# Attention and SiLU feed-forward in one kernel: output-weight rows regrouped, and the second batch's products moved into the first slab's second pass

## The chip, the cores and the metric

The kernel runs on one core of one Trainium2 chip. The metric is the device time of one launch in microseconds (us). Five engines work side by side, each on its own queue in program order: TensorE (PE in the profile, with its weight loads as PEld), VectorE (DVE), ScalarE (ACT), GpSimd (POOL) and SyncE (SP), which here only issues transfers. Sixteen DMA engines move the data.

## The reference, cut to what matters

```
q_s = exp(q) / sum over d            # 8 batches, 8 heads, 576 tokens, 64 wide
k_s = exp(k) / sum over tokens
kv  = k_s^T v                        # per batch and head, 64 x 64
x   = q_s kv, heads side by side     # 4608 tokens x 512
h   = x @ w_in                       # 512 x 2048
g   = h * sigmoid(beta * h)          # beta: one number for each of 2048 units
out = g @ w_out                      # 2048 x 512
```

(The maxima that the reference subtracts ahead of each exponential cancel in the quotients, and the kernel leaves them out.) All inputs and the output are float32; the matmuls run in bf16.

## The kernel before, in words

**Slabs and passes.** The 4608 tokens are nine slabs of 512. Slab t below 8 holds the first 512 tokens of batch t; slab 8 collects the last 64 of all batches. For each slab, pass 1 computes the hidden units: 16 tiles f of 128 units, each four matmuls over m (the four head pairs, 128 of the 512 features), 64 matmuls into PSUM banks 0 to 2 in turn. ACT turns each tile into GT with SiLU. Pass 2 multiplies GT with the output weights WOUT: four token groups u of 128, 16 matmuls each, again 64. The copies to O2S (`o2_evac`) and one store of 1 MB follow.

**Attention of a batch.** Heads are handled in pairs hp = 0 to 3. ACT makes EQ = exp(q) and EK = exp(k), where the two heads of a pair lie on partitions 0 to 63 and 64 to 127, so EK takes two instructions for each pair. DVE sums and scales EQ (`norm_main`, its product sometimes on POOL). PE transposes EQ into QT (`t_steps`; from batch 2 on a DMA does it). V is cast to bf16 in VB (`cast_v`). PE multiplies EK with VB over nine groups of 64 tokens (`kv_steps` or `kv_now`, nine matmuls for each pair); DVE scales the result by the reciprocal key sums into KVD (`kvd`); PE multiplies KVD with QT (`out_mm`), and the copy of that (`out_now`, `out_step`) is XT, which pass 1 of the batch's slab reads.

**How order is set.** Instructions are recorded once, in the order of the program, and each engine runs its own in that order. `Program.plan` derives semaphore waits from named keys (a tile's part, a PSUM bank). Attention of later batches is laid between the matmuls of the passes by hand: `tick()` counts matmuls in `slot`, and a list `todo` of pairs (tick, step) is worked off as the count passes. In slab 0 ticks 9 to 64 are pass 1 and ticks 65 to 128 are pass 2; `spread(steps, lo, hi)` distributes steps over ticks. Every matmul is recorded by `mm`, so all carry its line, L349, and can be told apart by their tiles: XT,WIN is pass 1, WOUT,GT pass 2, VB,EK the k-v products, QT,KVD and QTR,KVD the attention outputs (the latter for the 64 remaining tokens of two batches), IDB,EQ a transpose (L347), WARM a matmul on zeros that occupies PE during the head.

**The head.** SP issues q of batch 0 in four parts, beta, k and v in four parts each (L251, L522, L261). POOL issues the input weights in eight chunks of 256 columns, cast to bf16 by the transfer (`load_win`, L547), the first once k's third part has landed. Then come the output weights in four loads of 1 MB (`load_wout`, L532), gated by `wgate`: SP waits until W_in's chunk 4 of 0 to 7 has landed. They are staged as float32 in WST and O2S, and DVE scales them by 1/beta (RB) into WOUT (`scale_wout`). After them SP issues q, k and v of batch 1 in four parts each, the remaining q rows (QRF) and batch 2.

**Slab 0, pass 2.** The four token groups advance together, f by f, in banks 3 to 6. Batch 1's transposes of one pair each stand at ticks 109, 113, 117 and 121, its k-v products of pair 0 at tick 125. The other three pairs, the out matmuls and the copies of groups 0 and 1 follow behind pass 2, mixed with the first three tiles of slab 1 (`first_tiles`).

**Slab 1.** ACT makes the exponentials of batches 2 and 3 while PE runs pass 2; batch 2's k-v steps stand at ticks 97 to 108 and its outs at 112 to 124 (`attn_late`).

Of the kernel before, what the change touches and what calls it, by code (L numbers as in the profile page):

```python
# [14 lines left out]
D = 64  # L15
# [12 lines left out]
HS = S * D  # L28

# [127 lines left out]
def bass_efficient_attn_shen__then__act_swish_beta_kernel(  # L157
# [12 lines left out]
    with ExitStack() as es:  # L170
        def sb(name, shape, dt):
# [28 lines left out]
        BT = sb("BT", [NF, 128], F32)  # L200
# [4 lines left out]
        IDF = sb("IDF", [NF, NF], F32)  # L205
# [18 lines left out]
        add(POOL, lambda e: e.tensor_scalar(IDF[:, :], IOTA[0:NF, 0:NF], 0.0, None, ALU.is_equal),  # L224
            r=["iota"], w=["idf"])
        add(ACTE, lambda e: e.activation(DUMMY[:, 0:1], WARM[:, 0:1], ACT.Exp), r=["warm"],
            w=["dummy"])
# [10 lines left out]
        homes(0)  # L238

# [7 lines left out]
        def load_main(name, th, bufs, b, split=1):  # L247
            i = b % 2
            n = H // split
            for c in range(split):  # L250
                add(SP, lambda e, c=c: e.dma_start(dst(bufs[i], c * n, n), src(th, b, c * n, n)),  # L251
                    w=[(name, i, hp) for hp in range(c * n // 2, (c + 1) * n // 2)],
                    slot=f"{name}{i}_{c}")

        def load_pairs(name, th, bufs, b, split=1):
            i = b % 2
            n = NHP // split
            for c in range(split):
# [12 lines left out]
        def load_k(b, split=1):  # L271
            load_pairs("kf", kt_h, KF, b, split)

        def load_v(b, split=1):
            load_pairs("vf", vt_h, VF, b, split)
# [7 lines left out]


# [8 lines left out]
        def exp_k(b, hp0=0, n=4, step=1):  # L293
            i = b % 2
            for hp in range(hp0, hp0 + n, step):
                hps = range(hp, hp + step)
                for e_ in range(2):
# [5 lines left out]
                        r=[("kf", i, h) for h in hps], w=[("ek", i, h, e_) for h in hps])  # L303

# [26 lines left out]
        def cast_v(b, hp, eng=POOL):  # L331
            i = b % 2
            o = bass.AP(VB[i], hp * NG * VW, [[NHP * NG * VW, 128], [VW, NG], [1, 64]])
            a = bass.AP(VF[i], hp * KW, [[NHP * KW, 128], [64, NG], [1, 64]])
            add(eng, lambda e: (e.copy if eng == ACTE else e.tensor_copy)(o, a),  # L335
                r=[("vf", i, hp), ("vone", i)], w=[("vb", i, hp)])
# [133 lines left out]
        def attn_late(b):  # L470
            s = spread(kv_steps(b, (0, 1, 2, 3)), 97, 108)
# [3 lines left out]
            return s + spread(x, 112, 124)  # L475
# [17 lines left out]
        def ksum_inv(b, kb):  # L493
            i = b % 2
            add(DVE, lambda e: e.reciprocal(RC[i][:, :], PS[kb][:, 0:NHP]), r=[("ps", kb)],
                w=[("rc", i, hp) for hp in range(NHP)], bank=[kb])

        def kv_now(b, hp, bk, ks):
            i = b % 2
            for j in range(NG):  # L500
                l, r_, ke, kv, ko = kv_rows(b, hp, j)
                mm(PS[bk][:, 0:D + ks], l, r_[:, 0:D + ks], j == 0, j == NG - 1,
                   r=ke + kv + ko, w=[("ps", bk)], bk=bk)
            if ks:
                add(DVE, lambda e: e.reciprocal(RC[i][:, hp:hp + 1], PS[bk][:, D:D + 1]),
                    r=[("ps", bk)], w=[("rc", i, hp)], bank=[bk])
            kvd(b, hp, bk, 0)
# [8 lines left out]
        def go(steps):  # L516
# [4 lines left out]
        load_main("qf", qt_h, QF, 0, split=4)  # L521
        add(SP, lambda e: e.dma_start(BT[:, :], bass.AP(beta_h, 0, [[128, NF], [1, 128]])),  # L522
            w=["bt"], slot="bt")
        load_k(0, 4)
        load_v(0, 4)
# [4 lines left out]
        def load_wout(c):  # L530
            a = bass.AP(wout_h, 512 * c * DM, [[DM, 128], [128 * DM, 4], [1, DM]])
            add(SP, lambda e: e.dma_start(STAGE[c][:, :, :], a), w=SKEY[c],  # L532
# [12 lines left out]
        def load_win(c):  # L545
            a = bass.AP(win_h, 256 * c, [[DFF, 128], [128 * DFF, NM], [1, 256]])
            add(POOL, lambda e, c=c, a=a: e.dma_start(WIN[:, :, 256 * c:256 * c + 256], a),  # L547
                w=[("win", c)], slot=f"win{c}", after=P.writer[("kf", 0, 2)] if c == 0 else ())
            if c == 4:
                wgate.append(P.ops[-1])  # L550

        def read_beta():
            bb = bank(HEAD)
            mm(PS[bb][:, 0:NF], BT[:, :], IDF[:, :], True, True, r=["bt", "idf"],
               w=[("ps", bb)], bk=bb, tr=True)
            add(DVE, lambda e: e.tensor_scalar(BC[:, :], PS[bb][:, 0:NF], -1e-20, None,
                                               ALU.is_gt),
                r=[("ps", bb)], w=["bc0"], bank=[bb])
            add(DVE, lambda e: e.scalar_tensor_tensor(BC[:, :], PS[bb][:, 0:NF], 1e-20, BC[:, :],
# [3 lines left out]
                                                      PS[bb][:, 0:NF], ALU.mult, ALU.add),  # L563
                r=["bc", ("ps", bb)], w=["beta"], bank=[bb])
            add(DVE, lambda e: e.reciprocal(RB[:, :], BETA[:, :]), r=["beta"], w=["rb"])

        warm(8, 0)
# [4 lines left out]
        load_win(1)  # L572
# [5 lines left out]
        for c in range(2, 8):  # L578
            load_win(c)
        homes(1)  # L580
        exp_k(0)
# [7 lines left out]
        read_beta()  # L589
        cast_v(0, 0, DVE)  # L590
        warm(2, 0)
        ksum(0, 2, kb)
        cast_v(0, 1, DVE)
        go(t_steps(0, (3,), HEAD))
        warm(1, 0)
        ksum(0, 3, kb)
        ksum_inv(0, kb)
        cast_v(0, 2, ACTE)
        cast_v(0, 3, ACTE)
        warm(1, 0)  # L600
        add(ACTE, lambda e: e.activation(DUMMY[:, 1:2], WARM[:, 0:1], ACT.Silu), r=["warm"],
            w=["dummy"])

        hrot = [0]
        orot = [0]

        def pass1_mm(t, f, m, bk):
            x = XT8 if t == 8 else XT[t % 2]
            rd = [("xt8", p_) for p_ in range(4)] if t == 8 else [("xt", t % 2, m)]
            mm(PS[bk][:, :], WIN[:, m, 128 * f:128 * f + 128], x[:, m, :], m == 0,  # L610
               m == NM - 1, r=rd + [("win", f // 2)], w=[("ps", bk)], bk=bk)
# [4 lines left out]

        def first_tiles(t, n):
            bks = [HB[(hrot[0] + k) % 3] for k in range(n)]
            hrot[0] += n
# [194 lines left out]
```

## Time and profile before

| | us |
|---|---|
| median of 7 runs | 290.8 |
| lowest and highest of them | 290.34, 1037.62 |
| the profiled execution | 290.88 |
| its span | 289.05 |
| PE busy | 277.4 (96%) |
| ACT, DVE, POOL busy | 180.9, 111.8, 40.9 |
| first XT,WIN matmul | 16.69 |
| first WOUT,GT matmul of slab 0, of slab 1 | 30.71, 63.99 |
| last O2S copy begins | 285.22 |

Times inside the profile count from the span's start. PE is the engine that is nearly always busy, so what matters is where it isn't: idle time of another engine costs nothing by itself. A group's line gives its count, total and mean duration in ns, then the idle time of the engine before it and what ended it. In the timeline, the bracket at a line's end names the wait before it and its releaser. DMA queue q1 carries what SP and ACT issue, q0 what POOL issues, and q8 instruction fetches.

### The profile page before, as it was taken

How to read it: one execution, taken by the hardware profiler on the slowest of the kernel's cores; microseconds unless marked ns; L12 is line 12 of the kernel's file. 1: busy time of each engine (PE TensorE's matmuls, PEld its weight loads, DVE VectorE, ACT ScalarE, POOL GpSimd, SP SyncE). 2: the span in 40 equal slices, each digit the busy share in tenths (PEclk: the TensorE clock that was granted, in tenths of full speed). 3: DMA queues.
4: the chain of work that ended last, by engine and by line, in shares of the span. 5: the costliest groups of instructions: out<-in, count | busy, mean ns of one | idle time of the engine just before them, and what ended most of it. 6: DMA issues, size and time to landing. Idle time of an engine off the chain costs nothing.

```text
span 289.1 us, 3858 instructions
## 1 busy us (share of the span) xinstructions
PE 277.4 (96%) x1563; PEld 130.5 (45%) x1594; DVE 111.8 (39%) x205; ACT 180.9 (63%) x247; POOL 40.9 (14%) x60
## 2 busy tenths in 40 slices
PE   6889998999999999999999999999999999999994
PEld 2544443344444444444454445444544444444441
DVE  4731596207675157304660555054804300110011
ACT  5988469789987973689278926892660076017500
POOL 5770013033504030400040000000000000000000
PEclk9999999999999999999999999999999999999999
DMA  6999999995799999905990015000810030012022
GB/s 208 311 178 323 382 379 292 404 384 142 185 383 237 373 327 397 84 0 160 371 214 1 2 80 137 2 1 42 181 16 0 0 147 0 0 65 83 0 73 73
DMA packets 44306, 47.97 MB, mean 166 GB/s; under 512 B 20208, under 2 KB 32512, under 8 KB 43264
## 3 DMA queue, kind: packets, MB, share of 16 engines
q1 hardware_dynamic: 39744, 45.10, 50.7%
q0 software_dynamic: 4224, 2.10, 5.6%
q10 hardware_dynamic: 320, 0.52, 0.5%
q8 instruction: 12, 0.20, 0.3%
q14 instruction: 6, 0.05, 0.1%
HBM read 36.71 MB, written 9.44 MB: 160 GB/s over the span
## 4 chain that ended last, share of the span: by engine, by line
PE 77%; DMA 8%; SPq 6%; ACT 3%; issue 2%; POOL 2%; DVE 1%
PE PS L349 77%; DMA VF<-in_v_dram 4%; SPq L251 3%; DMA WIN<-in_moe_w_in_dram 2%; DMA KF<-in_k_dram 2%; SPq L261 2%; ACT EK L302 2%; SPq L532 1%; POOL WIN L547 1%; ACT EQ L290 1%; DVE O2S L650 0%; ACT L307 0%; POOL EQ L319 0%; DVE KVD L386 0%; ACT GT L613 0%
## 5 line engine op out<-in xcount | busy, mean ns | idle before, releaser
L613 ACT ACTIVATE GT<-PS,BETA 128x512 bf16<-128x512 f32 x144 | 98.3, 687 | 79.4 <-PE PS L349 79.3
L349 PE MATMUL PS<-XT,WIN 128*128 128x512 bf16 x562 | 130.8, 379 | 1.2 <-ACT XT L512 0.4
L349 PE MATMUL PS<-WOUT,GT 128*128 128x512 bf16 x562 | 131.2, 379 | 0.7
L349 PEld LDWEIGHTS PS<-XT,WIN 128*128 128x128 bf16 x576 | 55.4, 98 | 64.9 <-ACT GT L613 1.0
L349 PEld LDWEIGHTS PS<-WOUT,GT 128*128 128x128 bf16 x576 | 54.3, 98 | 62.4 <-DVE O2S L650 0.2
L650 DVE COPY O2S<-PS 128x512 f32<-128x512 f32 x34 | 23.2, 686 | 111.3 <-PE PS L349 111.3
L302 ACT ACTIVATE EK<-KF 64x1152 bf16<-64x1152 f32 (+1 forms) x40 | 38.7, 967 | 1.2 <-DMA KF<-in_k_dram 0.2
L349 PE MATMUL PS<-VB,EK 128*128 128x65 bf16 (+2 forms) x324 | 37.2, 190 | 2.0 <-POOL VB L335 1.0
L335 POOL CAST VB<-VF 128x576 bf16<-128x576 f32 x28 | 20.9, 745 | 74.6 <-PE PS L349 41.6
L349 PEld LDWEIGHTS PS<-VB,EK 128*128 128x128 bf16 x324 | 22.8, 97 | 10.0 <-POOL VB L335 2.3
L290 ACT ACTIVATE EQ<-QF 128x512 bf16<-128x512 f32 x32 | 18.2, 620 | 8.5 <-DMA QF<-in_q_dram 8.0
L317 DVE TENSOR_REDUCE QS<-EQ 128x8 f32<-128x512 bf16 (+1 forms) x22 | 20.1, 916 | 3.3 <-ACT EQ L290 3.1
L424 DVE CAST XT<-PS 128x512 bf16<-128x512 f32 x23 | 15.8, 691 | 11.5 <-PE PS L349 11.5
L319 DVE TENSOR_TENSOR EQ<-EQ,QI 128x1024 bf16<-128x1024 bf16 (+1 forms) x15 | 16.2, 1077 | 0.5
L349 PE MATMUL PS<-QT,KVD 128*128 128x512 bf16 x30 | 11.4, 380 | 0.5 <-DVE KVD L386 0.4
L319 POOL TENSOR_TENSOR EQ<-EQ,QI 128x512 bf16<-128x512 bf16 x7 | 7.3, 1044 | 31.4 <-DVE QI L318 31.2
L349 PE MATMUL PS<-WARM 128*128 128x512 bf16 x20 | 8.6, 548 | 1.2 <-DVE WARM L219 1.2
L386 DVE TENSOR_TENSOR KVD<-PS,RC 64x64 bf16<-64x64 f32 (+1 forms) x28 | 8.6, 308 | 1.1 <-PE PS L349 0.3
L325 DVE TENSOR_REDUCE QRS<-EQR 128x8 f32<-128x512 bf16 x4 | 2.7, 679 | 14.1 <-ACT EQR L307 14.1
L537 DVE TENSOR_SCALAR WOUT<-WST,RB 128x512 bf16<-128x512 f32 x8 | 3.3, 482 | 12.2 <-DMA WST<-in_moe_w_out_dram 12.2
L547 POOL DMA_DIRECT2D WIN<-in_moe_w_in_dram x8 | 6.2, 799 | 2.2 <-DMA KF<-in_k_dram 2.2
L290 ACT ACT_TABLE_LOAD x5 | 6.4, 1283 | 0.1
(47 smaller groups left out, 73.0 us busy)
## 6 DMA issues: line engine op xcount, KB each, us to landing
out_dram<-O2S SPq DMA_DIRECT2D x8, 1024.0 KB, 5.5
KF<-in_k_dram SPq DMA_DIRECT2D x6, 1152.0 KB, 8.9
VF<-in_v_dram SPq DMA_DIRECT2D x6, 1152.0 KB, 11.0
QF<-in_q_dram SPq DMA_DIRECT2D x6, 1024.0 KB, 7.8
KF<-in_k_dram SPq DMA_DIRECT2D x8, 288.0 KB, 7.6
VF<-in_v_dram SPq DMA_DIRECT2D x8, 288.0 KB, 8.4
QF<-in_q_dram SPq DMA_DIRECT2D x8, 256.0 KB, 7.0
WIN<-in_moe_w_in_dram POOLq DMA_DIRECT2D x8, 256.0 KB, 6.7
```

The source lines that it names most:

```text
L251: add(SP, lambda e, c=c: e.dma_start(dst(bufs[i], c * n, n), src(th, b, c * n, n)), w=[(name, i, hp) for hp in range(c * n // 2, (c + 1) * ...
L290: add(ACTE, lambda e, o=o, a=a: e.activation(o, a, ACT.Exp), r=[("qf", i, hp)], w=[("eq", i, hp)])
L302: add(ACTE, lambda e, o=o, a=a: e.activation(o, a, ACT.Exp), r=[("kf", i, h) for h in hps], w=[("ek", i, h, e_) for h in hps])
L317: add(DVE, lambda e: e.tensor_reduce(s_, a, AX.X, ALU.add), r=ks, w=[("qs", i, hp0)])
L319: add(eng, lambda e: e.tensor_tensor(a, a, vb, ALU.mult), r=ks + [("qi", i, hp0)], w=ks)
L335: add(eng, lambda e: (e.copy if eng == ACTE else e.tensor_copy)(o, a), r=[("vf", i, hp), ("vone", i)], w=[("vb", i, hp)])
L349: add(PE, lambda e: e.matmul(o, l, r_, start=start, stop=stop), r=r, w=w, bank=[bk])
L386: add(DVE, lambda e, o=o, a=a, s_=s_: e.tensor_tensor(o, a, s_, ALU.mult), r=[("ps", bk)] + [("rc", i, h) for h in hps], w=[("kvd", i, h, ...
L424: add(eng, lambda e: (e.copy if eng == ACTE else e.tensor_copy)(XT[i][:, hp, :], PS[bk][:, :]), r=[("ps", bk)], w=[("xt", i, hp)], bank=[bk])
L547: add(POOL, lambda e, c=c, a=a: e.dma_start(WIN[:, :, 256 * c:256 * c + 256], a), w=[("win", c)], slot=f"win{c}", after=P.writer[("kf", 0, ...
L613: add(ACTE, lambda e: e.activation(GT[:, f, :], PS[bk][:, :], ACT.Silu, scale=BETA[:, f:f + 1]), r=[("ps", bk), "beta"], w=[("gt", f)], ba ...
L650: add(eng, lambda e: (e.copy if eng == ACTE else e.tensor_copy)(O2S[t % 2][:, u, :], PS[bk][:, :]), r=[("ps", bk)], w=[("o2", t % 2, u)], ...
```

## The change

1. **W_out rows.** `load_wout` reads rows of w_out that lie together: 2 neighbouring rows (4 KB) to a partition in the first load, 4 rows (8 KB) in the other three. Partition p then holds the hidden units n p + k of a group in place of 128 k + p. The hidden units are therefore permuted everywhere: pass 1 takes every second or fourth column of WIN as its weights, and beta is turned to match (BT becomes two small tiles, six transposes in `turn_beta`, read later in `read_beta`).
2. **W_in chunks.** Five in place of eight: 256, 256, 512, 512, 512 columns. `wgate` waits for chunk 3, the fourth of the five.
3. **The head.** k of batch 0 is issued ahead of beta. The exponentials of k's pairs 2 and 3 become one instruction for each partition half, pairs 0 and 1 keep four; v's pairs 0 and 1 are cast by one DVE instruction. The k-v products of two pairs share a bank and a scaling; key sums of pairs 2 and 3 and the beta operations come later on DVE, and the outputs of pairs 2 and 3 are copied by DVE. The first tiles use other banks (`HFIRST`).
4. **Batch 1.** Its k and v parts are issued as k01, v01, k23, v23, and its exponentials cover two pairs each. All of its transposes (two pairs at a time, at ticks 103 and 111), its k-v products (pairs 0 and 1 at 105 to 109, 2 and 3 at 119 to 123) and three of its four outs (113, 117, 127) lie inside pass 2 of slab 0.
5. **Pass 2 of slab 0.** For f below 8 the four token groups advance together; then groups 0 and 1 run through f 8 to 15, then 2 and 3. The copies of 0 and 1 are recorded on ACT at ticks 113 and 114.
6. **Slab 1.** The remaining-token outs stand at 97 to 101, batch 2's k-v steps at 99 to 103 and 105 to 109 with two scalings, its outs at 110 to 123.

The diff, cut to its core:

```diff
+FG = {2: (0, 256), 4: (512, 1024, 1536)}
+WCH = ((0, 256), (256, 256), (512, 512), (1024, 512), (1536, 512))
...
+        def exp_kh(b, hp, n, e_):
+            i = b % 2
+            o = bass.AP(EK[i], 64 * e_ * NHP * NG * 128 + hp * NG * 128 + 64 * e_,
+                        [[NHP * NG * 128, 64], [128, NG * n], [1, 64]])
+            a = bass.AP(KF[i], 64 * e_ * NHP * KW + hp * KW,
+                        [[NHP * KW, 64], [64, NG * n], [1, 64]])
+            hps = range(hp, hp + n)
+            add(ACTE, lambda e: e.activation(o, a, ACT.Exp),
+                r=[("kf", i, h) for h in hps], w=[("ek", i, h, e_) for h in hps])
...
         def attn_late(b):
-            s = spread(kv_steps(b, (0, 1, 2, 3)), 97, 108)
+            s = spread(kv_steps(b, (0, 1)), 99, 103) + spread(kv_steps(b, (2, 3)), 105, 109)
...
-            return s + spread(x, 112, 124)
+            return s + spread(x, 110, 123)
...
+        def kv_mm(b, hp, bk, n):
             for j in range(NG):
                 l, r_, ke, kv, ko = kv_rows(b, hp, j)
-                mm(PS[bk][:, 0:D + ks], l, r_[:, 0:D + ks], j == 0, j == NG - 1,
-                   r=ke + kv + ko, w=[("ps", bk)], bk=bk)
...
+                mm(PS[bk][:, VW * n:VW * n + D], l, r_[:, 0:D], j == 0, j == NG - 1,
+                   r=ke + kv, w=[("ps", bk)], bk=bk)
...
         def load_wout(c):
-            a = bass.AP(wout_h, 512 * c * DM, [[DM, 128], [128 * DM, 4], [1, DM]])
-            add(SP, lambda e: e.dma_start(STAGE[c][:, :, :], a), w=SKEY[c],
+            n = 2 if c == 0 else 4
+            a = bass.AP(wout_h, 512 * c * DM, [[n * DM, 128], [128 * n * DM, 4 // n], [1, n * DM]])
+            o = bass.AP(STAGE[c], 0, [[4 * DM, 128], [n * DM, 4 // n], [1, n * DM]])
+            add(SP, lambda e: e.dma_start(o, a), w=SKEY[c],
                 slot=f"wst{c}", after=wgate if c == 0 else ())
...
         def load_win(c):
-            a = bass.AP(win_h, 256 * c, [[DFF, 128], [128 * DFF, NM], [1, 256]])
-            add(POOL, lambda e, c=c, a=a: e.dma_start(WIN[:, :, 256 * c:256 * c + 256], a),
+            c0, n = WCH[c]
+            a = bass.AP(win_h, c0, [[DFF, 128], [128 * DFF, NM], [1, n]])
+            add(POOL, lambda e, c0=c0, n=n, a=a: e.dma_start(WIN[:, :, c0:c0 + n], a),
                 w=[("win", c)], slot=f"win{c}", after=P.writer[("kf", 0, 2)] if c == 0 else ())
-            if c == 4:
+            if c == 3:
                 wgate.append(P.ops[-1])
...
         def pass1_mm(t, f, m, bk):
...
-            mm(PS[bk][:, :], WIN[:, m, 128 * f:128 * f + 128], x[:, m, :], m == 0,
-               m == NM - 1, r=rd + [("win", f // 2)], w=[("ps", bk)], bk=bk)
+            n = 2 if f < 4 else 4
+            l = bass.AP(WIN, m * DFF + 128 * (f // n * n) + f % n, [[NM * DFF, 128], [n, 128]])
+            mm(PS[bk][:, :], l, x[:, m, :], m == 0, m == NM - 1,
...
+        HFIRST = ((0, 1, 2, 4, 6, 7, 0, 1, 2, 7), (3, 4, 0, 1, 2, 5, 0, 1, 2))
+
+        def hbank(t, f):
+            return HFIRST[t][f] if t < 2 and f < len(HFIRST[t]) else HB[f % 3]
...
+            if t == 0:
+                order = [(f, u) for f in range(NF // 2) for u in us]
+                order += [(f, u) for h in (us[0:2], us[2:4]) for f in range(NF // 2, NF) for u in h]
...
-                todo = [(109 + 4 * hp, lambda hp=hp: go(t_steps(1, (hp,), (7, 1, 2))))
-                        for hp in range(NHP)] + [(125, lambda: kv_now(1, 0, 0, 1))]
+                todo = [(TT[k_], lambda k_=k_: go(t_steps(1, (2 * k_, 2 * k_ + 1), (1 + k_,))))
+                        for k_ in range(2)]
+                todo += [(113, lambda: o2_evac(0, 0, 3, ACTE)), (114, lambda: o2_evac(0, 1, 4, ACTE))]
+                todo.append((127, lambda: out_now(1, 2, 2, DVE)))
+                todo.append((100, lambda: norm_main(1, 3, 1)))
+                todo += spread(kv_steps(1, (0, 1), (0,)), 105, 109)
+                todo += [(113, lambda: out_now(1, 0, 7, DVE)), (117, lambda: out_now(1, 1, 1, ACTE))]
+                todo += spread(kv_steps(1, (2, 3), (0,)), 119, 123)
             elif t == 1:
-                todo = spread(outr_steps(1), 99, 104) + attn_late(2)
+                todo = spread(outr_steps(1), 97, 101) + attn_late(2)
...
-                load_k(1, 4)
-                load_v(1, 4)
+                load_k(1, 4, (0, 1))
+                load_v(1, 4, (0, 1))
+                load_k(1, 4, (2, 3))
+                load_v(1, 4, (2, 3))
                 load_qrem(0)
                 load(2)
                 exp_q(1)
...
-                exp_k(1)
+                for hp in (0, 2):
+                    exp_kh(1, hp, 2, 0)
+                    exp_kh(1, hp, 2, 1)
+                add(ACTE, lambda e: e.activation(DUMMY[:, 2:3], WARM[:, 0:1], ACT.Silu),
+                    r=["warm"], w=["dummy"])
...
-                o2_evac(0, 0, 3, ACTE)
-                kv_now(1, 1, 1, 1)
-                o2_evac(0, 1, 4, ACTE)
-                kv_now(1, 2, 2, 1)
-                out_now(1, 0, 3, ACTE)
-                kv_now(1, 3, 7, 1)
                 at = first_tiles(1, FIRST[1])
-                out_now(1, 1, 4, ACTE)
                 at(0)
-                out_now(1, 2, 3, DVE)
+                out_now(1, 3, 7, ACTE)
                 at(1)
```

## The prediction

> **What bounds the kernel now.** I read the page first, then the chain of waits, then the timeline engine by engine between 12 and 82 us, then the DMA traffic in short windows.
>
> ```profile
> span 289.1 us, 3858 instructions
> PE   6889998999999999999999999999999999999994
> DMA  6999999995799999905990015000810030012022
> ```
>
> TensorE (PE) is full from about 20 us on. Each slice is 7.2 us; the two places where PE falls off are the head (to 20 us) and the slice at 43 to 51 us. The DMA row is full over the same first 45 us, so what PE lacks there is data. The chain says it piece by piece (start, length, what):
>
> ```profile
> 36.04 11.59 DMA VF<-in_v_dram
> 47.63 0.05 issue
> 47.68 0.68 POOL VB L335
> 48.36 0.05 issue
> 48.41 1.75 PE PS L349 x15
> ...
> 52.02 0.70 ACT GT L613
> ```
>
> Batch 1's last V lands at 47.63, GpSimd casts it, PE follows; at 52.02 PE waits for a bank that the first GT evacuation frees. The timeline, by engine:
>
> ```profile
> 31.41 2.72 SPq L261 DMA_DIRECT2D KF<-in_k_dram  x4
> 34.17 2.30 SPq L261 DMA_DIRECT2D VF<-in_v_dram  x4
> 41.35 5.63 ACT L302 ACTIVATE EK<-KF 64x576 bf16<-64x576 f32 x8
> 44.48 0.66 POOL L335 CAST VB<-VF 128x576 bf16<-128x576 f32 x1 [2.92 <-DMA VF<-in_v_dram]
> 52.76 11.40 PE L349 MATMUL PS<-XT,WIN 128*128 128x512 bf16 x51 [0.35 <-ACT GT L613]
> 63.99 7.29 PE L349 MATMUL PS<-WOUT,GT 128*128 128x512 bf16 x33
> ```
>
> Slab 0 enters pass 2 at 30.71 and slab 1 enters it at 63.99. At 0.2155 us per 512-wide matmul (the 52 between 52.76 and 63.99 take 11.23), the work between is 128 matmuls (27.6), 16 transposes (0.9), 36 k-v matmuls (33 ns each, 1.2) and 4 out matmuls (0.9), 30.6 us in all. It took 33.3, so 2.7 us of stall is all that can be won there.
>
> Landings, from issue plus the time to landing in the DMA view of single issues: K pairs 0 and 1 at 41.3 and 42.05, pairs 2 and 3 at 42.9 and 43.6, V at 44.5, 45.85, 46.8, 47.6.
>
> **Part 1: the transfers.** All of batch 1 queues behind both weight matrices, so their speed sets its landings. Queue lines from four windows, 14 to 17, 20 to 22.5, 28 to 34 and 230 to 238 us (packets, MB, share of 16 engines):
>
> ```profile
> q0 software_dynamic: 999, 0.50, 126.7%
> q0 software_dynamic: 988, 0.49, 145.2%
> q1 hardware_dynamic: 1167, 2.32, 104.2%
> q1 hardware_dynamic: 144, 1.05, 32.0%
> ```
>
> W_in's packets (1 KB read, 512 B written) go at 333 to 395 per us, 48 to 40.5 ns each on 16 engines. W_out's 2 KB packets take 16 x 6 / 1135 = 84.6 ns. The last line is an output store in 8 KB packets: 0.32 x 16 x 8 us / 128 = 320 ns, 410 GB/s.
> - W_in: three quarters of it become half as many packets of 2 KB read. No row shows that form. Ends: twice the small packet, 96 ns (gain 0), and 77 ns (estimate: 81 less one saved packet overhead). I take 81, nearest the 84.6 row: 1584 x 81 / 16 = 8.0 us against 3168 x 44 / 16 = 8.7. Gain 0.7 (0 to 1.1).
> - W_out: 10.7 us now at 390 GB/s. By the store row 10.2. The Trainium skill (DMA: Bandwidth & Descriptors, Specifications) gives a fabric ceiling of 435 GB/s; at that it would be 9.6, a gain of 1.1. The store is the same row length on the same engines, so I stay near it: 0.6.
> - The gate: the first W_out load waits for W_in chunk 3 of 5, three quarters of the matrix, where it waited for five eighths. Before, SP issued at 21.40 and the first q1 packets came near 23.5 with W_in still flowing until 24.4, so no hole. After, chunk 3 lands near 22.1, first packets near 24.2, W_in ends near 23.5. If the 2.1 us was only queueing behind W_in the hole is 0, otherwise 0.7. I take 0.35.
> Sum: batch 1 lands 0.7 + 0.6 - 0.35 = 0.95 us earlier (0 to 1.7).
>
> GpSimd now issues the second W_in chunk after the EQ multiply (1.06 us), about 12.1 instead of 11.06; the first chunk's packets last until 14.0, so it is covered. Chunk 2 should land near 19.7 and is needed at 20.7.
>
> **Part 2: batch 1's products.** PE is in order. The token-pair matmuls before tick 105 are 41; with 8 transposes PE is there near 41.3 (from pass 2 at about 31.0, and the transposes wait for EQ pair 1 off GpSimd, 41.6 now, 0.95 earlier then). There the k-v matmuls of pairs 0 and 1 need both wide exponentials and two V casts. K pair 1 lands at 42.05 - 0.95 = 41.1; two 64x1152 ACT instructions (1.18 each by slab 1's row, 4 in 4.71) end at 43.45. V pair 1 takes the place of K pair 3 in the queue: 43.6 - 0.95 + 0.69 = 43.35. So PE resumes at X = 43.5, and everything queued behind waits too, 23 ready pass-2 matmuls among it.
> From X: 23 matmuls 4.96, 36 k-v 1.2, 8 transposes 0.46, 3 outs 0.65, then slab 1's pass 1 with its one out 14.0, and 0.15 for KVD ahead of the out at tick 127 (estimate from the 0.44 us KVD rows). Slab 1 enters pass 2 at X + 21.4 = 64.9, against 63.99: **+0.9**. The bank stall at 52 is gone inside that sum, since f 3 to 5 get their own banks. K and V pairs 2 and 3, landing 45.85 and 47.6 less 0.95, plus casts or two exponentials, are ready near 47.4, when PE reaches tick 119 (X + 4.5): no second wait. ACT then has the table load and the two O2S copies; banks 3 and 4 come free near 49.9, before slab 1 asks at 50.8.
>
> **Part 3: the head.** Removed: 3 warm matmuls; added: 5 small transposes. K issues move up 0.5 us, but the queue is full, so landings stay. V pair 1 (12.06) gates the double cast, ending 13.4; then one cast, the QT copy, KVD pair (two of about 0.3), RC, four beta operations (0.85), KVD, two XT copies on DVE (0.69 each): 18.5, against 18.1 for the last XT before. So pass 1 runs about 0.3 later (-0.5 to +1). Cost nothing: PE waits until X anyway. If X came early, this is paid in full.
>
> **Part 4: strided weights.** All 576 loads of WIN now step 2 or 4 elements. The row:
>
> ```profile
> L349 PEld LDWEIGHTS PS<-XT,WIN 128*128 128x128 bf16 x576 | 55.4, 98 | 64.9 <-ACT GT L613 1.0
> ```
>
> 98 ns contiguous, beside a 216 ns matmul; it may double and stay hidden. Against the change speaks the Trainium skill's Advanced Engine Details and Errata, SBUF Cachelines: lines of 16 bytes, and at least two hits on each are needed to hide the access. A step of 4 bf16 gives exactly two, so by the rule nothing is lost; a load four times as long would cost (392 - 216) x 544, some 96 us. Nothing here shows a strided load. I take 0.
>
> **Part 5: slab 1's pass 2.** The k-v steps move up and the outs spread; the 0.4 us wait on KVD at 76.8 and a shorter one at 73.7 go. What is late next: XT pair 3, copied by ACT behind sixteen us of exponentials:
>
> ```profile
> 80.89 0.59 ACT L424 CAST XT<-PS 128x512 bf16<-128x512 f32 x1
> ```
>
> It ends 81.48; the fourth matmul of slab 2 used it at 81.77. So only **-0.28** is won. Later slabs keep their instructions; f % 3 banks meet no busy bank there.
>
> **Sum:** +0.9 - 0.28 = +0.65 us on the profiled execution, 290.88 (span 289.05 and 1.8 around it). The median of the runs is 290.8, so 291.5.
>
> **Rivals.**
> - *The wait moves into pass 2* (likeliest): as summed, +0.2 to +1.7 with the transfer bounds. For it: K cannot be there at tick 105, which PE reaches before 41.5.
> - *K slips past an instruction fetch*, ending faster. Q pair 2 lands at 38.6 and pair 3 at 40.6, where 0.8 apart is usual; between, at 37.8 to 38, stands this packet:
>
> ```profile
> q8 instruction: 1, 0.02, 33.9%
> ```
>
>  A third of 16 x 0.2 us: one engine was held 1.08 us, and everything behind it stays late. K pair 1's data ends near 39.3 now. If the transfers win 1.5 us or more instead of 0.95, it ends before the fetch: K lands at 39.25, exponentials end at 41.6, and V pair 1, cast at 42.8 for the second half of the products, makes X worth about 42.05: -0.75 us, 290.1; with still faster transfers 289.3. Against it: it needs nearly all bounds of part 1 at their good ends, and no hole at the gate.
> - *Nothing measurable*: transfers 1.1 to 1.4 us earlier give X near 43.1 and +0.3 or less; 290.9.
> - *It does not drain early*: the O2S copies stand on ACT behind the exponentials of pairs 2 and 3 and the table load, so the pair is free near 50, not at tick 113. That costs nothing and gains nothing; it is in every case above.
> - *Strided loads show*: tens of us. Rule and cover speak against it.
>
> **Numbers.** About 0.2% is what a measurement of this kernel tells from no change, 0.58 us. Chances: wait in pass 2 0.59, of which 0.46 beyond 0.2% and 0.13 within; nothing measurable 0.05; fetch escaped 0.32; strided loads 0.04. So faster 0.32, same 0.18, slower 0.50. The range takes 289.3 from the escape and 292.6 from late transfers; the likeliest case alone is 291.0 to 292.6.
>
> **What would show it.** Right: PE stands before the first VB,EK matmul of slab 0's pass 2 until 43 to 44 us, released by ACT EK or POOL VB; no ACT GT release at 52; slab 1's first WOUT matmul near 64.9; WIN's LDWEIGHTS near 98 ns; W_out's first packets near 24. Wrong: K pair 1 landing before 40, that first WOUT matmul before 63.5, or a WIN matmul pitch above 0.216.

## Result, and the profile after

The changed kernel takes 294.5 us (median of 12 runs, 291.38 to 295.13), the kernel before 290.79 (31 runs, taken beside it; one of them took 1037.62 us, and no trace of it was kept): a ratio of 1.0116, interval 1.0093 to 1.0139. It is slower, as forecast most likely, but by 3.7 us and not by 0.7, and outside the range. The profiled execution took 294.33 us; its span is 3.48 us longer than that of before. The clock row of before, and the page of the changed kernel:

```profile
PEclk9999999999999999999999999999999999999999
```

```profile
span 292.5 us, 3843 instructions
PE   5889959999999999999999999999999999999994
PEclk9799997999999999999999999999999999999998
DMA  6999999996599999904890007000720030002022
```

The dent in the PE row is in the sixth slice now (36.6 to 43.9 us). The row that the prediction never looked at is PEclk: before it was 9 in all slices; here the slice after the dent has a 7. (The other 7, in the second slice, is a fall in the head, from 7.4 to 10.8; pass 1 began at 16.14 all the same, 0.55 earlier than before.) The timeline of TensorE (start, length, what; in the bracket the idle time before, and what ended it):

```profile
41.78 0.40 PE L360 MATMUL PS<-IDB,EQ 128*128 128x128 bf16 x4 [1.62 <-POOL EQ L331]
42.02 0.59 PE L362 MATMUL PS<-WOUT,GT 128*128 128x512 bf16 x2
44.27 0.19 PE L362 MATMUL PS<-VB,EK 128*128 128x65 bf16 x1 [1.66 <-ACT EK L314]
...
67.56 7.07 PE L362 MATMUL PS<-WOUT,GT 128*128 128x512 bf16 x32
...
83.40 0.81 PE L362 MATMUL PS<-XT,WIN 128*128 128x512 bf16 x3
84.88 0.39 PE L362 MATMUL PS<-XT,WIN 128*128 128x512 bf16 x1 [0.67 <-ACT XT L437]
```

The forecast wait is there, at the forecast place, with the forecast releaser: PE stands before the first VB,EK matmul. But X is 44.27, not 43.5. The 67.56 is the second matmul of slab 1's pass 2, because the record of the first is missing. The weight loads (PEld), before and after, show it:

```profile
63.78 0.74 PEld L349 LDWEIGHTS PS<-WOUT,GT 128*128 128x128 bf16 x4
```

```profile
67.13 0.96 PEld L362 LDWEIGHTS PS<-WOUT,GT 128*128 128x128 bf16 x5
```

Before, the first WOUT,GT matmul starts 0.21 behind its load, at 63.99; here that is 67.35. So slab 1 enters pass 2 at X + 23.08, and not at X + 21.4 (it is X + 21.44 in the executions at full clock below). The windows of 1 us around X tell where the other 1.64 us went (busy time of each engine with its instructions, then the granted TensorE clock, the DMA share, GB/s):

```profile
43.00:44.00 1.00, 0.00 (x0) 0.00 (x0) 0.97 (x3) 1.00 (x1) 0.87 (x2) 1.00 1.07 396
44.00:45.00 1.00, 0.73 (x12) 0.52 (x12) 0.43 (x1) 0.37 (x2) 0.36 (x1) 0.98 1.23 263
45.00:46.00 1.00, 1.00 (x12) 0.55 (x9) 0.00 (x0) 0.98 (x2) 0.28 (x1) 0.50 1.22 208
46.00:47.00 1.00, 1.00 (x7) 0.51 (x6) 0.39 (x2) 1.00 (x1) 0.49 (x2) 0.50 1.15 270
47.00:48.00 1.00, 1.00 (x9) 0.81 (x8) 0.35 (x2) 0.98 (x2) 0.56 (x1) 0.50 1.10 305
48.00:49.00 1.00, 1.00 (x6) 0.48 (x5) 0.69 (x1) 0.99 (x4) 0.00 (x0) 0.81 1.11 355
49.00:50.00 1.00, 0.95 (x6) 0.45 (x5) 0.69 (x1) 0.58 (x2) 0.00 (x0) 1.00 1.07 382
```

PE has work again from 44.3, at half the clock from about 45 until past 48: 0.04 + 3 + 0.38 of the windows, 3.4 us in all, of which half, 1.7, is what a full PE would lose. That is what is missing. The whole adds up to the span: slab 1's pass 2 begins 3.36 later (1.72 from X, 1.64 from the clock), slab 2's fourth matmul comes 17.53 behind it in place of 17.78 (-0.25), and from that matmul to the end it is 207.65 in place of 207.28 (+0.37). Sum +3.48.

### The profile page after: what moved, and what is told of

It reads as the page before. It is cut to its first block, busy times and chain, and to the rows that moved or that the text cites. A ratio compares the mean times of both kernels' runs of the same rounds, so it can differ in the third digit from the quotient of the medians.

```text
span 292.5 us, 3843 instructions
## 1 busy us (share of the span) xinstructions
PE 277.9 (95%) x1565; PEld 137.0 (47%) x1596; DVE 111.1 (38%) x198; ACT 178.0 (61%) x239; POOL 39.1 (13%) x57
## 4 chain that ended last, share of the span: by engine, by line
PE 82%; DMA 7%; SPq 3%; POOL 2%; issue 2%; ACT 1%; DVE 1%; POOLq 0%; ACTq 0%
PE PS L362 82%; DMA WIN<-in_moe_w_in_dram 3%; DMA KF<-in_k_dram 3%; SPq L259 2%; SPq L249 1%; DMA QF<-in_q_dram 1%; POOL WIN L559 1%; ACT EK L314 1%; POOL EQ L331 1%; SPq L543 1%; DVE QS L329 0%; PE PS L360 0%; DVE EQ L331 0%; DVE O2S L684 0%; ACT GT L635 0%
## 5 line engine op out<-in xcount | busy, mean ns | idle before, releaser
L362 PE MATMUL PS<-WOUT,GT 128*128 128x512 bf16 x562 | 133.4, 381 | 0.6
L362 PEld LDWEIGHTS PS<-XT,WIN 128*128 128x128 bf16 x576 | 62.2, 109 | 60.8 <-ACT XT L437 1.2
L362 PEld LDWEIGHTS PS<-VB,EK 128*128 128x128 bf16 x324 | 23.9, 100 | 10.8 <-issue 3.3
L304 ACT ACTIVATE EK<-KF 64x1152 bf16<-64x1152 f32 x24 | 27.8, 1158 | 0.4
L314 ACT ACTIVATE EK<-KF 64x1152 bf16<-64x1152 f32 (+1 forms) x10 | 9.5, 966 | 2.7 <-DMA KF<-in_k_dram 2.6
L399 DVE TENSOR_TENSOR KVD<-PS,RC 64x128 bf16<-64x128 f32 (+1 forms) x22 | 7.7, 349 | 1.2 <-PE PS L362 0.5
L360 PE MATMUL PS<-IDB,EQ 128*128 128x128 bf16 x32 | 3.9, 265 | 4.4 <-POOL EQ L331 2.9
L362 PE MATMUL PS<-WARM 128*128 128x512 bf16 x17 | 6.8, 536 | 1.2 <-DVE WARM L221 1.2
```

Source lines behind the costliest of these rows:

```text
L304: add(ACTE, lambda e, o=o, a=a: e.activation(o, a, ACT.Exp), r=[("kf", i, h) for h in hps], w=[("ek", i, h, e_) for h in hps])
L314: add(ACTE, lambda e: e.activation(o, a, ACT.Exp), r=[("kf", i, h) for h in hps], w=[("ek", i, h, e_) for h in hps])
L362: add(PE, lambda e: e.matmul(o, l, r_, start=start, stop=stop), r=r, w=w, bank=[bk])
L399: add(DVE, lambda e, o=o, a=a, s_=s_: e.tensor_tensor(o, a, s_, ALU.mult), r=[("ps", bk)] + [("rc", i, h) for h in hps], w=[("kvd", i, h, ...
```

## The experiments

The kernel before was run beside each group, and its medians lay from 290.79 to 291.25. X is the start of the first VB,EK matmul of slab 0's pass 2, "slab 1" the start of slab 1's pass 2; both are from the profiled execution. (Four executions, those with a clock of 0.50, lack the record of slab 1's first WOUT,GT matmul; their start is taken from the weight loads, as above.)

| kernel | median us (runs) | ratio to before | X | slab 1 | clock after X |
|---|---|---|---|---|---|
| the change | 294.5 (12) | 1.0116, 1.0093 to 1.0139 | 44.27 | 67.35 | 0.50 |
| e1 fill 7 and 7 | 294.37 (4) | 1.0101, 1.0058 to 1.0145 | 45.32 | 66.76 | 1.00 |
| e2 late products | 290.99 (12) | 0.9998, 0.9976 to 1.0021 | no wait | 63.67 | 1.00 |
| e3 old batch 1 | 291.4 (12) | 1.0018, 0.9997 to 1.0039 | no wait | 64.83 | 1.00 |
| e4 old rows | 295.32 (4) | 1.013, 1.0079 to 1.0182 | 44.70 | 68.47 | 0.50 |
| e5 old slab 1 | 294.61 (5) | 1.009, 1.0057 to 1.0123 | 44.33 | 67.40 | 0.50 |
| e6 e5 with fill | 293.29 (8) | 1.0071, 1.0044 to 1.0098 | 43.89 | 65.34 | 1.00 |
| e7 e2, unit step | 290.47 (21) | 0.9979, 0.9967 to 0.999 | no wait | 63.29 | 1.00 |
| e8 e2, old rows, DVE | 290.87 (21) | 0.9998, 0.9981 to 1.0016 | no wait | 65.68 | 1.00 |
| e9 early gate | 292.31 (15) | 1.0042, 1.002 to 1.0064 | 43.44 | 64.87 | 1.00 |
| e10 late, tuned | 290.8 (14) | 0.999, 0.9973 to 1.0008 | no wait | 64.36 | 1.00 |
| e11 e10, early gate | 289.92 (22) | 0.9958, 0.9939 to 0.9978 | no wait | 64.72 | 1.00 |
| e12 fill 5 and 6 | 293.55 (6) | 1.0079, 1.0056 to 1.0103 | 45.78 | 67.22 | 1.00 |
| e13 the change again | 294.55 (8) | 1.0095, 1.0062 to 1.0127 | 44.75 | 67.79 | 0.50 |
| e14 fill 7 and 7 | 293.71 (7) | 1.0091, 1.0059 to 1.0123 | 44.87 | 66.31 | 1.00 |

**Which part of the change loses the time: e2, e3, e4.** e2 keeps everything but moves batch 1's products late in pass 2 and behind it (with other banks for slab 1's first tiles); e3 puts batch 1 and pass 2 of slab 0 back to where they were before (points 4 and 5 of the change); e4 puts the weight rows, chunks and columns back and keeps the rest.

```diff
 # e2
-        TT = (103, 111)
+        TT = (112, 117)
-                todo += spread(kv_steps(1, (0, 1), (0,)), 105, 109)
+                todo += spread(kv_steps(1, (0, 1), (0,)), 119, 123)
...
 # e3: the todo list of slab 0 and what follows pass 2 as before
-                todo += spread(kv_steps(1, (0, 1), (0,)), 105, 109)
...
+                        for hp in range(NHP)] + [(125, lambda: go(kv_steps(1, (0,), (0,))))]
...
 # e4
-WCH = ((0, 256), (256, 256), (512, 512), (1024, 512), (1536, 512))
+WCH = tuple((256 * c, 256) for c in range(8))
...
-            n = 2 if c == 0 else 4
+            n = 1
```

> The kernel after, with batch 1's steps moved back to where their data is there: transposes at ticks 112 and 117, products of pairs 0 and 1 at 119 to 123, the first out at 127, and pairs 2 and 3 with the other outs behind pass 2. Rows of the weights, gate, head and slab 1 stay. Theory 1: no wait above 1 us in pass 2 and a clock of 1.00; slab 1 enters pass 2 near 63.0 and the time is 289.5 (289 to 290.5), under the kernel before. Theory 2: most of the loss stays, 293 or more.

> The kernel after, with only the move of batch 1 undone: transposes of one pair at ticks 109 to 121, pair 0's products at 125, the rest behind pass 2, token groups together, k and v parts and exponentials in the old order. Rows, gate, head and slab 1 stay as after. Theory 1: 291 (290.3 to 291.7), about the kernel before. Theory 2: 294.

> The kernel after, with the weights' rows undone: 2 KB rows of w_out, eight chunks of W_in, the gate on chunk 4 of 0 to 7, contiguous weight columns, beta in one tile. The move of batch 1 stays. Theory 1: the wait at tick 105 stays within 0.7 us of the kernel after and the clock falls again: 294 to 295. Theory 2: 291 or less.

With the products late or back in their old place the loss is gone (e2 290.99, e3 291.4); with the old rows it is all there (e4 295.32). So the early products make the loss, and the rows don't. e2's timeline; it waits 0.71 us for EQ, which it transposes, where the change has two waits of 3.3 us together:

```profile
44.16 0.40 PE L360 MATMUL PS<-IDB,EQ 128*128 128x128 bf16 x4 [0.71 <-DVE EQ L331]
...
44.82 0.19 PE L362 MATMUL PS<-VB,EK 128*128 128x65 bf16 x1
```

The first product is at 44.82, later than X in the change, and it costs nothing, because PE worked off its pass-2 matmuls in the meantime. e2 did not reach its 289.5: it has waits of 0.72 (W_in's third chunk), 0.57 (a copy in slab 1's first tiles) and 0.62 (the ACT copy of XT) of its own.

**Is the rest the clock: e1, e5, e6, e12, e13, e14.** The fill puts matmuls on zeros (WARM) into PE's two idles and changes nothing else in the program. e5 and e6 leave out point 6 of the change.

```diff
 # e1, e14 (and e6 on top of e5); e12 with 5 and 6
+                todo += [(102.5, lambda: warm(7, 7)), (104.5, lambda: warm(7, 7))]
...
 # e5, e6: point 6 of the change undone
-            s = spread(kv_steps(b, (0, 1)), 99, 103) + spread(kv_steps(b, (2, 3)), 105, 109)
+            s = spread(kv_steps(b, (0, 1, 2, 3)), 97, 108)
...
-            return s + spread(x, 110, 123)
+            return s + spread(x, 112, 124)
```

> The kernel after, with seven matmuls on zeros (1.5 us) laid ahead of the transposes at tick 103 and seven more ahead of the first k-v product at tick 105; they fill the two idle stretches of TensorE there (1.6 and 1.7 us) and nothing else waits for them. Theory 1 (TensorE's wait costs twice: the idle time, and the halved clock that follows it from 45 to 48.4 us): the wait stays, the clock row stays at 1.00 behind it, and 3.4 us at half speed, that is 1.7 us, come back: 292.8 against 294.5. Theory 2 (the weights' rows, the stepped weight loads or the later gate make the kernel slower, and the clock is beside the point): 294.5, unchanged.

> Only point 6 of the change is undone: slab 1's k-v steps, outs and remaining-token outs go back to the ticks of before. Theory 1 (PE's early wait for batch 1 costs its length and then the halved clock): the wait and the half clock stay, slab 1 enters pass 2 at 67.0 to 68.7 as with the whole change, and the 0.46 us that point 6 won comes back: 294.9, span 292.9. Theory 2 (slab 1's new order is itself a loss): the time falls below 294.

> As e5_old_slab1, and 14 matmuls on zeros stand at ticks 102.5 and 104.5 of slab 0's pass 2, in PE's early wait. Theory 1: the granted clock stays 1.00 at 44 to 49 us, slab 1 enters pass 2 21.4 us after the first VB,EK matmul and not 23.3, and the time is 1.8 us below e5_old_slab1: about 293.1. Theory 2 (the clock's share is something else, or is lost again at the next wait): within 0.4 us of e5_old_slab1. If W_in or K land at other times in the profiled execution, the distance from the first VB,EK matmul to slab 1's pass 2 decides.

> The whole change with 5 and 6 matmuls on zeros (1.08 and 1.30 us) in PE's two early idles of 1.62 and 1.66 us, so that the fill is shorter than the waits and can't set the first product's time itself, as 7 and 7 could. Theory 1 (the clock falls because the two idles follow closely, and its fall costs 1.85 us of the median): clock 1.00 from 44 to 49 us, slab 1 enters pass 2 21.4 us after the first VB,EK matmul, and the median falls to 292.5 to 293.0. Theory 2 (most executions behind the median don't lose the clock, and only the profiled ones do): median within 0.5 of 294.5, as e1_warm_in_wait's was.

> The whole change, unaltered, beside e14_fill_same_chip on one chip: 294.5, and the clock at 0.5 after the early wait. It is the reference for e14.

> e1_warm_in_wait's edit (7 and 7 matmuls on zeros in the two idles), on the same chip as e13_change_same_chip. Theory 1 (nearly every execution loses the clock, at 1.85 us): the median lies 1.5 to 2.0 below e13's. Theory 2 (the clock falls in part of the executions, or its loss is partly covered by a later wait): 0.3 to 1.2 below. No difference would mean that the half clock is made up for later, and that the wait's length alone is the loss.

In the traces it is plain: without fill the distance from X to slab 1's pass 2 is 23.08, 23.07 and 23.04 us (the change, e5, e13), with it 21.44, 21.45, 21.44 and 21.44 (e1, e6, e12, e14). That is 1.60 to 1.64 for the clock; the 1.85 and the 23.3 of the expectations were read from the second matmul. First the changed kernel on the chip of e13 and e14, then the filled one:

```profile
44.75 0.21 PE L362 MATMUL PS<-VB,EK 128*128 128x65 bf16 x1 [2.40 <-ACT EK L314]
44.78 0.61 PE L362 MATMUL PS<-WOUT,GT 128*128 128x512 bf16 x1
...
68.00 2.32 PE L362 MATMUL PS<-WOUT,GT 128*128 128x512 bf16 x10
```

```profile
44.87 0.19 PE L362 MATMUL PS<-VB,EK 128*128 128x65 bf16 x1 [0.72 <-ACT EK L314]
44.90 0.38 PE L362 MATMUL PS<-WOUT,GT 128*128 128x512 bf16 x1
...
66.31 4.05 PE L362 MATMUL PS<-WOUT,GT 128*128 128x512 bf16 x18
...
80.80 0.39 PE L362 MATMUL PS<-QT,KVD 128*128 128x512 bf16 x1 [1.07 <-DMA QT<-EQ]
```

The same wide matmul takes 0.61 in the one and 0.38 in the other, and slab 1's pass 2 begins 1.48 earlier (66.31 for 67.79) though X is 0.12 later. The times of all runs give back less: by the medians 0.84 (e13 to e14, in the range of its theory 2), 1.3 (e5 to e6), 0.95 (the change to e12, on other chips) and 0.1 (the change to e1), by the means 0.17 and 0.74 for the first two pairs; in each pair the two intervals overlap. Of the expected times e6's came (293.29 for 293.1); e1's and e12's did not. Part of the reason is that X came about 0.5 later on average in the four filled executions than in the three without fill. For e1 and e14 the second trace shows another part: PE now waits 1.07 us (1.15 in e1) for the DMA transposes of batch 2's QT, a wait that the kernel without fill doesn't have. In exactly these two an instruction fetch falls between the issue and the landing of those transposes, at 78.0 to 78.5 in e14 and half a microsecond later in e1; in e5, e6, e12 and the change it comes after 82:

```profile
q1 hardware_dynamic: 389, 0.10, 108.5%
q8 instruction: 1, 0.02, 11.3%
```

11.3% of 16 engines for 0.5 us is one engine held for 0.9 us, and the transposes issued last take 4.5 us to landing with it, 3.2 in e13. So the half clock is shown as a cost of 1.6 us between X and slab 1, in the traces; how much of the 3.7 in the medians it makes is not settled, 0.8 to 1.3 by the medians of the two pairs that shared a chip. Executions without a trace have their mean clock on record, and one fall of 3.4 us takes 0.006 of it. In all 29 runs of the four kernels that leave both idles open (the change, e4, e5, e13) it is 0.994 or less; with fill it is 0.996 or more in 6 of 25. The head can have a fall of its own, so the mean does not say where the clock fell, but none of the 29 ran without a fall.

e5 gives a value for point 6. Its slab 2 has its fourth matmul 17.76 behind slab 1's pass 2, where the change has 17.53: 0.23 us, and not the 0.46 of its expectation, which started from the second matmul. The median of e5 (294.61) is too rough to show that.

**What makes the clock fall.** The length of one idle does not tell. In each of the twelve traces with more than one half-clock stretch, they begin whole multiples of 3.41 us apart (in the change at 7.41, at 44.96, which is 11 of them later, and at 290.72, 72 later) and last 3.41 us or twice that, unless the kernel ends. Cut into stretches of 3.41 us in that phase, the sixteen traces have 1249 from 17 us on. PE was busy for 0.83 to 1.52 us in the five that a half clock followed, and for 1.91 us or more in the 1244 others. Below are two stretches of the change, the one before its fall and the fall itself, then one of e8 (columns as above, PE's busy time the second number):

```profile
41.55:44.96 3.41, 1.51 (x17) 0.82 (x18) 2.81 (x5) 2.53 (x3) 1.96 (x3) 1.00 1.10 359
44.96:48.37 3.41, 3.41 (x27) 2.11 (x25) 0.84 (x4) 3.37 (x3) 1.33 (x2) 0.50 1.15 269
```

```profile
42.97:46.39 3.42, 1.92 (x17) 1.17 (x18) 3.28 (x7) 2.51 (x3) 2.33 (x3) 1.00 1.13 325
```

e8 has idles of 1.60 and 0.71 us there, close together, and keeps its clock, since a border at 42.97 lies inside the first. The position of the borders differs from one execution to the next (in the change one lies 0.69 us behind X, in e13 0.02 ahead of it), so by these figures the same idles could cost the clock in one and not in another; no two executions here show that. Between 1.52 and 1.91 us of work in 3.41 nothing was measured. In the head, where transposes, short products and matmuls on zeros make up PE's work, busy time alone does not tell (in e7 the clock fell behind a stretch with 2.87 us); why stays open.

**Was the early wait's length mis-sized by the gate: e9.**

```diff
-            if c == 3:
+            if c == 2:
                 wgate.append(P.ops[-1])
```

> The whole change, but the first load of W_out waits for W_in's chunk 2 (half of the matrix) and not for chunk 3. Theory 1 (the gate leaves the DMA engines nearly empty at 24 to 25.5 us, and batch 1 lands that much later): SP issues the first load near 21.2 in place of 23.45, no slice without traffic follows, the scales of W_out start 0.7 to 1.2 us earlier (28.0 or so), the first VB,EK matmul of slab 0's pass 2 comes near 43.3 in place of 44.27, and the time falls by about 1: 293.4. The halved clock stays. Theory 2 (W_out is only slowed by what is left of W_in): landings and X move by less than 0.4 and the time stays within 0.4 of 294.4.

The time fell by more than expected, to 292.31, and X came at 43.44 as expected, but not in the expected way. SP issued at 21.03, yet W_out shared the engines with W_in's rest: its first scaling began at 29.00 (28.96 in the change) and its fourth at 36.34 (36.48). K of pairs 0 and 1 was there 0.8 earlier, but that lies within what executions with the same transfers scatter (see the last section), so the gate isn't shown as its cause. PE's timeline:

```profile
21.06 7.10 PE L362 MATMUL PS<-XT,WIN 128*128 128x512 bf16 x32 [0.60 <-DMA WIN<-in_moe_w_in_dram]
28.82 3.65 PE L362 MATMUL PS<-XT,WIN 128*128 128x512 bf16 x16 [0.66 <-DMA WIN<-in_moe_w_in_dram]
...
41.64 0.40 PE L360 MATMUL PS<-IDB,EQ 128*128 128x128 bf16 x4 [0.54 <-POOL EQ L331]
...
43.44 0.19 PE L362 MATMUL PS<-VB,EK 128*128 128x65 bf16 x1 [0.97 <-ACT EK L314]
...
64.87 5.34 PE L362 MATMUL PS<-WOUT,GT 128*128 128x512 bf16 x24
```

PE stands for W_in's last chunk at 28.8, enters pass 2 1.0 later than in the change (32.30 for 31.27), and so finds shorter idles at the products, 0.54 and 0.97. With those the clock did not fall (1.00 in every window from 44 to 50), and slab 1's pass 2 is X + 21.43. In this execution, idle time in an earlier place cost nothing, and the clock was kept; the medians of the two kernels are 2.2 apart, and their intervals do not meet.

**The stepped weights: e7.**

```diff
-            l = bass.AP(WIN, m * DFF + 128 * (f // n * n) + f % n, [[NM * DFF, 128], [n, 128]])
+            l = bass.AP(WIN, m * DFF + 128 * f, [[NM * DFF, 128], [1, 128]])
```

> e2_late_products with WIN's columns taken side by side as PE's weights; the hidden units are then paired with other units' output rows, so the output is not the reference's. Theory 1 (steps of 2 and 4 elements slow the loads a little: 109 ns against 98, 0.35 us over slabs 2 to 8): LDWEIGHTS 98 ns, 207.3 us from slab 2's fourth matmul to the end and not 207.7, time 0.3 to 0.4 below e2: 290.6. Theory 2 (the 0.35 us comes from something else): 207.7 us stay, time as e2, 291.0.

e7 leaves out the match of hidden units and output rows, so its output is not the reference's and only its time counts. From the groups of the two pages, the weight loads of WIN in the change and in e7:

```profile
L362 PEld LDWEIGHTS PS<-XT,WIN 128*128 128x128 bf16 x576 | 62.2, 109 | 60.8 <-ACT XT L437 1.2
```

```profile
L362 PEld LDWEIGHTS PS<-XT,WIN 128*128 128x128 bf16 x576 | 55.5, 98 | 65.6 <-DVE XT L520 2.4
```

98 ns in place of 109, and from slab 2's fourth matmul to the end 207.3 us in place of e2's 207.7. The median is 0.5 below e2's, taken on another chip. So the step costs about 0.35 us in all, though each load stays beside a 216 ns matmul.

**A version that is faster than both: e8, e10, e11.** e8 puts e2 on the old rows; e10 instead goes for e2's three own waits; e11 is e10 with the early gate.

```diff
 # e8 and e10
-                x += out_step(b, hp, MB, ACTE if hp == 3 else DVE)
+                x += out_step(b, hp, MB, DVE)
 # e10, on e2
-WCH = ((0, 256), (256, 256), (512, 512), (1024, 512), (1536, 512))
+WCH = ((0, 256), (256, 256), (512, 256), (768, 256), (1024, 512), (1536, 512))
-        FIRST = (2, 3)
+        FIRST = (2, 4)
 # e11: the gate at chunk 3 of these 6, in e10 at chunk 4
```

> The late products of e2 on the old weight rows, chunks and columns (points 1 and 2 undone), and batch 2's last XT copied by DVE in place of ACT. Theory 1: against e2 the weights' step gives back 0.35 us, the wait for W_in's third chunk in pass 1 (0.7) falls to about 0.2, the wait of 0.6 for XT at slab 2's start goes; against it the products at ticks 119 to 123 may wait 0.3 to 0.5 for K and V: 289.7, range 289.3 to 290.2, faster than both kernels. Theory 2 (the wider rows were a gain that this gives up): 290.8 or more.

> The late products of e2, with its three small waits addressed: W_in in six chunks (four of 256 columns, two of 512, so the first eight tiles step 2 elements and W_out's first two loads have 4 KB rows), four first tiles in slab 1 in place of three, and batch 2's last XT copied by DVE. From e2's trace: 0.72 at 20.8 falls to 0.2 or less, 0.57 at 51.1 to 0.15, 0.62 at 81.2 to 0: 289.6, range 289.2 to 290.3, faster than both kernels. If PE's waits are given back by K and V that land at their own time (as e8's did), 290.5 or more.

> As e10_late_tuned, and W_out's gate waits for chunk 3 of 6 (half of W_in). Batch 1 then lands about 1 us earlier, but the late products hardly wait for it: within 0.3 us of e10_late_tuned, with fewer high runs. If the tail chunks of W_in are slowed by W_out so that pass 1 waits for them, up to 0.8 more.

e8 and e10 missed their numbers (290.87 and 290.8). In e8's execution the first scaling of W_out began at 29.76 and batch 1 came late, so that slab 1 started pass 2 2.0 later than in e2; the wait for XT at slab 2 was gone. e10 lost the wait for W_in and the one at slab 2, kept the one for a copy in slab 1's first tiles (0.57), and got 0.41 and 0.66 for the transposes and 0.35 for QTR. Of the kernels that compute the reference, e11 is the only one clear of the kernel before: 289.92, ratio 0.9939 to 0.9978. It was expected level with e10 and is 0.9 below. Its profiled execution (290.73, 0.8 above its own median) has no shorter span than e10's (288.9 against 289.0), so why the medians differ stays open.

## Why the prediction was wrong, point by point

**What held.** The mechanism (PE reaches the products of batch 1 before their data, and stands with 23 ready matmuls behind), its place, its releaser ACT EK, no wait at 52 for a GT copy, the 21.4 us of work behind X (21.43 to 21.45 in the five executions at full clock), a head that costs nothing (pass 1 began 0.55 earlier, where 0.3 later was forecast, and PE waits until X anyway), no second wait at tick 119, and slab 1's gain with XT on ACT late next (-0.25 for -0.28).

**The step that failed: "Slab 1 enters pass 2 at X + 21.4".** Part 2 priced the wait by its length and let PE run at full speed after it. The clock has no term in the sum, and no rival has it. In the trace slab 1 enters pass 2 at X + 23.08: +1.64, the largest gap between forecast and measurement. The PEclk row of before is 9 in all slices; the sum took that for a constant. The idles were foreseen (the transposes' wait until near 41, X at 43.5): two of them, close together, were in the working. The Trainium skill (TensorE: Matmul & The Clock Gate, What's actually happening) says that the clock gate goes to half rate after an idle window of about 3.4 us, and back after a busy one as long; under HAM oscillation the rule is put as no idle gap over that. Here each gap is about half of that, and PE had worked 1.51 of the 3.41 us ahead of the fall; with gaps of 0.54 and 0.97 (e9) it had worked 2.44, and the clock held. By the rule for one gap the term would have been 0; by the table's half rate for 3.4 us it is an estimated 1.7, near the 1.64 measured.

**The term that was mis-sized: part 1's 0.95 us.** K of pairs 0 and 1 was there at 41.7, 0.35 earlier than before and not 0.95, and X 0.77 later than forecast. What follows compares one execution of each kernel. In nine executions with the transfers of the change, K's first exponential starts between 39.58 and 43.29; their median, 41.84, is that of the change (41.78) within 0.1, but the scatter of before is not known, so the split is no firmer than that.
- W_in: forecast gain 0.7, measured none. The packets are half as many at about the price forecast (16 / 207 us is 77 ns), but the small ones were cheaper in this window (16 / 394 us is 41 ns) than the 44 taken, so the bytes move hardly faster. The same window of 22 to 23 us, before and after (packets, MB, share):

```profile
q0 software_dynamic: 394, 0.20, 144.6%
```

```profile
q0 software_dynamic: 207, 0.21, 125.3%
```

 From 14 to 19 us both move 0.14 to 0.17 MB each microsecond. Chunk 3 landed at 23.4 where 22.1 was forecast, and the last chunk at 25.97 (25.41 before).
- The gate: forecast 0.35, measured about 1.0. SP issued at 23.45 in place of 21.40, and from 24 to 25 us the queues carried little:

```profile
q1 hardware_dynamic: 8, 0.03, 46.2%
q0 software_dynamic: 54, 0.05, 29.3%
```

 W_out's first scaling began at 28.96 in place of 28.16, although its megabyte took less time. (By e9, an earlier gate alone does not win that back.)
- W_out: forecast 0.6, measured 0.8. The scalings are 2.51 us apart in place of 2.72, 0.21 for each of four megabytes; from 27 to 30 us the queue moved 434 GB/s, more than the store row of 410 that the estimate leaned on, and near the ceiling of 435 that the prediction cites and didn't take.

 Together 0.8 - 1.0 is about -0.2 for W_out's end, and the fourth scaling is indeed 0.17 later than before (36.48 against 36.31). The 0.35 that K is earlier came in the q and k transfers behind it, for which no step had a term: both executions have one instruction fetch ahead of K's pair 1, and it cost 1.3 us before (q's pair 3 landed 2.05 behind pair 2, where 0.75 is usual) but 0.8 in the change (K's pair 1 landed 1.51 behind pair 0).

**The term set to 0: part 4.** The stepped loads cost 0.37 in the span. The rule of two hits on a 16-byte line, which the prediction takes from the Trainium skill (Advanced Engine Details and Errata, SBUF Cachelines), put the cost at nothing; the trace has 109 ns for 98. The measurement decides: small, but not 0.

**The rivals.** K ahead of the instruction fetch did not come in the change: the fetch is at 39.5 to 40 there, and K landed at 41.7. In e6 it did, with exponentials from 39.58 to 41.93, and it would not have paid as forecast: V was late instead, its casts ended at 43.18 (42.8 forecast), and the fill at 43.9.

**The sum**, as forecast and as measured: X +0.9 and +1.72, clock none and +1.64, slab 1 -0.28 and -0.25, stepped weights 0 and +0.37; +0.65 and +3.48.

## What to carry to other kernels

Work moved ahead in an engine that runs in order must have its data there at the new place, not only its slot: PE's own later matmuls were the cover for batch 1's landing, and the change put the products in front of that cover. Price an idle of PE twice, once for its length and once for the clock that comes after it: add up PE's work within any 3.4 us, and where 1.5 us or less of it is left, the clock can fall; where idle time can't be avoided, spread it over places that are apart. A row width is worth what the bytes per microsecond say, and not what the packet count says.

## What the hardware showed that was not expected

- The granted clock fell to 0.5 for 3.4 us after idles of only 1.3 to 2.4 us, in four of four executions that had two such idles (the change, e4, e5, e13; in e4 for 6.8); filled, or cut to 0.54 and 0.97, in none of five, nor with 1.60 and 0.71 (e8) or with 1.51 alone (e1, at 22 us). What told was PE's work within a stretch of 3.41 us: 1.52 or less and the clock fell, 1.91 or more and it held, outside the head.
- The transfer that casts W_in moved 0.20 to 0.21 MB each microsecond with 1 KB rows and with 2 KB rows; the plain load of W_out went from 390 to 434 GB/s with rows of 4 to 8 KB.
- A weight load with a step of 2 or 4 elements takes 109 ns in place of 98; with half of the tiles at step 2 and half at step 4 (e11) it is 106.
- One instruction fetch of 16 KB holds a DMA engine for about 1 us, and what it delays depends on where it falls: in two of the three kernels with 14 matmuls more it fell into a DMA transpose that PE waits for.
- Batch 1's data lands up to 3.7 us apart between executions of kernels whose transfers are the same: K's first exponential starts at 39.58 in e6 and at 43.29 in e12, and X was 44.27 and 44.75 in two executions of the change.
